# Token mixing in scaled float16 pairs, two of three score sets joined, and early blocks split 5, 4, 3

## The chip, the cores and the metric

One core of a Trainium2 chip runs the whole kernel. The metric is the time on the device in microseconds (us); the kernel before takes 724.33 us (median of three runs, 723.59 to 726.13).

## What is computed

Four batches of 576 tokens, eight heads of 64 channels. Forget-gated causal attention is followed by a mixer (over tokens, then over channels) and by a gated feed-forward with a convolution of three taps along the tokens. Cut to what matters:

```python
scores = q @ k.T / sqrt(64) + (cum[:, None] - cum[None, :])     # cum: running sum of log f; causal
attn = exp(scores - max) / (sum + 1e-9)
x = concat_heads(attn @ v)                                      # 4 x 576 x 512
h = relu(x.T @ w_tok1) @ w_tok2                                 # token mixing: 576 -> 256 -> 576
u = x + h.T
x2 = u + relu(u @ w_ch1) @ w_ch2                                # channel mixing: 512 -> 1536 -> 512
hh = relu(x2 @ w_in)                                            # 512 -> 1024
out = (hh * sigmoid(conv3(hh))) @ w_out
```

The weights come as float64 and are turned into float32 on the chip. The results have to hold to about float32, so most products are made of pairs: a value is split into a high and a low part of 16 bits (or of TensorE's reduced 32-bit format, float32r), and three matmuls (high by high, high by low, low by high) stand for one.

## The kernel before, in words

**The order is planned.** The program adds tasks (engine, estimated time, rank, what it reads and writes) to a list scheduler, `Order`. It takes, again and again, the task that can begin first by its estimates, and among those that can begin at once the one with the lowest rank. The result is one fixed order for each engine, and each engine then waits in that order for real. A rank is thus a priority. `PER` is the step of rank from one head to the next; weights, loads and groups have ranks relative to heads. Channel mixing on TensorE has a rank of 1000 and more, so it fills what the attention leaves free.

**Attention** (32 heads, `pair(p)` for two heads at a time, lines 1031 to 1088). `score` makes three sets of row blocks for both heads: block 4; blocks 0 and 3; blocks 1 and 2. Products of 64 rows in float32 are followed by one product that adds the decay. The result lies in the PSUM ring "z", which has two slots: the set of block 4 takes both (one per head), each other set takes one. VectorE's `smax` (line 912) reads a slot, adds the mask, takes the maximum and so frees it; ScalarE's `sexp` (line 918) makes the exponential. The first 8 heads and the last are transposed by TensorE (line 951), the others by the DMA from float16 pairs: GpSimd makes the high part (`ph`, line 927), VectorE the low part (`pl`, line 933). `pv` multiplies by v (line 983 in float32 for the first 8 heads, lines 988 to 990 in pairs later); `norm` and `xout` (lines 992 to 1007) give x.

**Token mixing** runs once for each group of 4 heads, 8 groups in all (`group(g)`, line 1169). ScalarE and GpSimd split x into `xh` and `xl` in float32r. `t1` makes two results with 15 matmuls of 256 columns each, `t1_hi` and `t1_lo` split them, and `t2` makes four results, each from three transposes of x (the residual, `t2_x`, line 1128) and six matmuls of 288 columns. ScalarE copies each to `us`. All pair matmuls go through the helper `mm3` (lines 278 to 280). The token weights go through `weight` (line 326): load, decode on ScalarE and VectorE (lines 315, 319, 320), a high part on ScalarE, a low part on GpSimd.

**Channel mixing.** After two groups a batch is complete: the largest of u (`um`), a scale (`su`), float16 pairs `uh` and `ul`, and then a first part of the 12 blocks of 128 hidden channels, `PARTS_M[0] = 4` of them, can run while attention goes on with the next batch. The parts of 5 and of 3 blocks, and the feed-forward, follow after attention. The weights of a part are loaded and decoded, their squares summed for a scale (`weight_set`, line 407) and split (lines 467 and 471). v is scaled from group 2 on by a power of two from the sum of its magnitudes (`v_abs`, `v_sum`, `v_pow`).

Of the kernel before, what the change touches and what calls it, by code (L numbers as in the profile page):

```python
# [143 lines left out]
def fox_moe_kernel(  # L144
# [14 lines left out]
    nc = tc.nc  # L159
# [35 lines left out]
    PARTS_M = (4, 5, 3)  # L195
# [13 lines left out]
    SETR = ((-25.0, 0.0),)  # L209
    LATER = (-60.0, 0.0, 20.0)  # L210
    PER = 5.0
# [112 lines left out]
    def weight(block, place, rank, key, pools_=(), copy=None):  # L324
# [51 lines left out]
        T("POOL", 0.1 + 1.3 * k, rank, low, reads=[c, (key, "h")], writes=[key], pools=pools_)  # L376

# [286 lines left out]
    with tc.manual_schedule():  # L664
# [114 lines left out]
        def v_abs(g):  # L779
# [7 lines left out]
        def v_sum(g):  # L787
            ps = bank("w")[:, 0:1]
            nc.tensor.matmul(ps, ones.to_broadcast([128, 128]), vs_t[g], start=True, stop=True)
            vps_t[g] = ps  # L790

        def v_pow(g):
            sc = ap1.tile([128, 2], F32, tag="vsc", name="vsc", bufs=3)
            nc.vector.tensor_scalar(sc[:, 0:1], vps_t[g], 2.0 ** -86, None, ALU.max)
            si = sc[:, 0:1].bitcast(I32)
            nc.vector.tensor_scalar(si, si, 0x7F800000, 0x7F800000, ALU.bitwise_xor, ALU.bitwise_and)
            nc.vector.tensor_scalar(sc[:, 0:1], sc[:, 0:1], 8192.0, None, ALU.mult)
            nc.vector.tensor_scalar(sc[:, 1:2], sc[:, 0:1], PSC * 1e-9, 2.0 ** -125, ALU.mult, ALU.max)
# [18 lines left out]

        def v_tasks(g, rank):
# [4 lines left out]
            if HG * g < FULL:  # L823
                if g:
                    T("SP", 2.0, rank - 6, load_v32, g, writes=keys, moved=3.0, pools=["a3"])
                return
# [3 lines left out]
            kw = turn("w")  # L830
            junk = ("junk",)
            T("ACT", 1.27, rank, v_abs, g, reads=[vf], writes=[junk, ("vacc", g % 2)], pools=A2)
            T("PE", 0.2, rank, v_sum, g, reads=[("vacc", g % 2)], writes=[kw], pools=["a1"], ring=[kw])
            T("DVE", 0.5, rank, v_pow, g, reads=[kw], writes=[("vsc", g % 3)], pools=["a1"], ring=[kw])
# [8 lines left out]
        w1h = ap1.tile([128, NS, TOK], F32R, tag="w1h", name="w1h", bufs=1)  # L843
        w1l = ap1.tile([128, NS, TOK], F32R, tag="w1l", name="w1l", bufs=1)
        nc.gpsimd.memset(f32(w1h[64:128, 0]), 0.0)
# [648 lines left out]
```

## Time and profile before

| | us |
|---|---|
| median of the runs (lowest to highest) | 724.33 (723.59 to 726.13) |
| the profiled execution, its own time | 724.63 |
| its span, first to last instruction | 722.9 |
| TensorE matmuls busy | 701.9 (97%) |
| VectorE busy | 507.7 (70%) |
| ScalarE busy | 418.0 (58%) |
| GpSimd busy | 214.2 (30%) |

In the profile PE is TensorE's matmul side, PEld its weight loads, DVE VectorE, ACT ScalarE, POOL GpSimd and SP the engine that issues the DMAs. The duration of a matmul in the trace includes its way through the array; consecutive matmuls overlap, and what one costs in a stream is the distance from its start to the next start.

### The profile page before, as it was taken

The page shows a single profiled execution, that of the slowest core. Times are in us where ns is not written, and L with a number is a line of the kernel's source. Part 1 is how long each engine was busy: PE and PEld are TensorE (multiplying, and loading weights), DVE is VectorE, ACT ScalarE, POOL GpSimd, SP SyncE. Part 2 cuts the span into 40 slices and gives each one's busy share as a digit, 9 for nine tenths or more (in the row PEclk, how much of TensorE's full clock was granted, in tenths as well). Part 3 has the DMA queues.
Part 4 walks back from the last instruction along what each step waited for, and adds up shares of the span by engine and source line. Part 5 has one row for each costly group of instructions (what it writes and reads, how often), then busy time and mean ns, then how long its engine had stood idle before and what let it go on. Part 6 is the DMA issues. An engine that isn't in the chain of part 4 may idle for free.

```text
span 722.9 us, 16264 instructions
## 1 busy us (share of the span) xinstructions
PE 701.9 (97%) x6399; PEld 570.5 (79%) x6399; DVE 507.7 (70%) x1226; ACT 418.0 (58%) x921; POOL 214.2 (30%) x272
## 2 busy tenths in 40 slices
PE   7999879999999999999999999999999999999998
PEld 6888857768787888878878787778877778778786
DVE  6778999899877795375758566335668866975570
ACT  6878685665756454476645443112168766776672
POOL 2351564564264541400001103011013323322230
PEclk9999999999999999999999999999999999999999
DMA  9546898998999597974557644054111111100101
GB/s 214 165 142 218 189 234 162 250 224 211 222 209 178 107 236 164 314 214 145 163 150 210 196 156 151 15 170 126 35 66 50 50 54 47 51 25 26 34 18 50
DMA packets 152973, 101.98 MB, mean 141 GB/s; under 512 B 89984, under 2 KB 145024, under 8 KB 152896
## 3 DMA queue, kind: packets, MB, share of 16 engines
q1 hardware_dynamic: 152896, 100.94, 54.2%
q8 instruction: 50, 0.82, 0.5%
q14 instruction: 27, 0.22, 0.1%
HBM read 57.73 MB, written 23.59 MB: 113 GB/s over the span
## 4 chain that ended last, share of the span: by engine, by line
PE 81%; DVE 11%; ACT 2%; issue 2%; DMA 1%; POOL 1%; SPq 0%; DVEq 0%; POOLq 0%; ACTq 0%
PE w L279 14%; PE w L278 14%; PE w L280 13%; PE z L279 9%; PE z L280 9%; PE z L278 9%; PE z L894 5%; DVE pl L933 3%; PE w L983 3%; DVE t L912 2%; PE w L1128 1%; DVE w L320 1%; PE z L898 1%; PE w L988 1%; PE w L989 1%
## 5 line engine op out<-in xcount | busy, mean ns | idle before, releaser
L278 PEld LDWEIGHTS <-w 128*128 128x128 f16 x1280 | 125.3, 98 | 35.3 <-issue 4.1
L280 PEld LDWEIGHTS <-w 128*128 128x128 f16 x1280 | 125.4, 98 | 34.0 <-issue 2.3
L279 PEld LDWEIGHTS <-w 128*128 128x128 f16 x1280 | 125.1, 98 | 31.2 <-issue 0.4
L279 PE MATMUL w<-ul,w 128*128 128x288 f16 x384 | 110.1, 287 | 2.1 <-DVE ul L510 2.1
L278 PE MATMUL w<-uh,w 128*128 128x288 f16 x384 | 110.0, 287 | 0.3 <-ACT uh L507 0.3
L280 PE MATMUL w<-uh,w 128*128 128x288 f16 x384 | 110.0, 286 | 0.0
L1394 DVE SCALAR_TENSOR_TENSOR cv<-hp,cw,cv 128x286 f32<-128x286 f32 (+1 forms) x128 | 75.0, 592 | 37.9 <-ACT cv L1388 35.6
L273 POOL TENSOR_TENSOR g<-sg,g 128x286 f16<-128x286 f32 (+1 forms) x64 | 55.1, 867 | 156.5 <-ACT g L267 154.8
L559 ACT ACTIVATE r<-w 128x288 f16<-128x288 f32 x96 | 39.1, 408 | 101.5 <-PE w L280 101.2
L918 ACT ACTIVATE t<-t,m 128x192 f32<-128x192 f32 (+4 forms) x160 | 81.3, 553 | 17.3 <-DVE m L912 16.6
L912 DVE CUSTOM_DVE_ANT_0 t<-z,mask 128x192 f32<-128x192 f32 (+4 forms) x160 | 70.3, 478 | 10.1 <-PE z L898 10.0
L563 DVE SCALAR_TENSOR_TENSOR r<-w,r 128x288 f16<-128x288 f32 x96 | 43.4, 454 | 45.9 <-ACT r L559 45.0
L279 PE MATMUL z<-g,w 128*128 128x286 f16 (+1 forms) x256 | 73.3, 286 | 0.0
L278 PE MATMUL w<-vh,w 128*128 128x288 f16 x256 | 73.2, 286 | 0.0
L279 PE MATMUL w<-vl,w 128*128 128x288 f16 x256 | 73.2, 286 | 0.0
L280 PE MATMUL w<-vh,w 128*128 128x288 f16 x256 | 73.2, 286 | 0.0
L278 PE MATMUL z<-r,w 128*128 128x288 f16 x256 | 73.2, 286 | 0.0
L279 PE MATMUL z<-r,w 128*128 128x288 f16 x256 | 73.2, 286 | 0.0
L280 PE MATMUL z<-r,w 128*128 128x288 f16 x256 | 73.2, 286 | 0.0
L278 PE MATMUL z<-g,w 128*128 128x286 f16 (+1 forms) x256 | 73.0, 285 | 0.0
L280 PE MATMUL z<-g,w 128*128 128x286 f16 (+1 forms) x256 | 72.9, 285 | 0.0
L636 POOL TENSOR_TENSOR p<-p,u 128x288 f32<-128x288 f32 x32 | 26.1, 847 | 157.3 <-DMA p<-p_d 90.8
(181 smaller groups left out, 1660.6 us busy)
## 6 DMA issues: line engine op xcount, KB each, us to landing
wraw<-in_moe_w_ch_dram SPq DMA_DIRECT2D x24, 512.0 KB, 4.7
qk<-in_qk_dram SPq DMA_DIRECT2D x16, 608.0 KB, 5.2
u_d<-us SPq DMA_DIRECT2D x8, 576.0 KB, 3.8
p_d<-res SPq DMA_DIRECT2D x32, 144.0 KB, 3.3
p<-p_d SPq DMA_DIRECT2D x8, 576.0 KB, 5.0
u<-u_d SPq DMA_DIRECT2D x8, 576.0 KB, 5.2
x_d<-p SPq DMA_DIRECT2D x8, 576.0 KB, 3.1
u<-x_d SPq DMA_DIRECT2D x8, 576.0 KB, 4.0
```

Of the source, the lines that this page charges most:

```text
L273: nc.gpsimd.tensor_tensor(o, a, b, ALU.subtract)
L278: nc.tensor.matmul(ps, wh, xh, start=(first and i == 0), stop=False)
L279: nc.tensor.matmul(ps, wh, xl, start=False, stop=False)
L280: nc.tensor.matmul(ps, wl, xh, start=False, stop=(last and i == n - 1))
L559: nc.scalar.activation(out=t[:, 0, :], in_=box["z", m], func=AF.Relu)
L563: nc.vector.scalar_tensor_tensor(t[:, 1, :], box["z", m], 0.0, f32(t[:, 0, :]), ALU.max, ALU.subtract)
L636: nc.gpsimd.tensor_tensor(box["p"][:, d], box["p"][:, d], box["u"][:, d], ALU.add)
L894: nc.tensor.matmul(out_[x], t[r, Q0[i]:Q0[i] + 128], t[r, k0:k0 + n], start=first, stop=False)
L912: nc.vector.tensor_tensor_reduce(to, z_t.pop((n, i)), mk, -0.125, 3e38, ALU.add, ALU.min, m_t[n][0:rows, i:i + 1])
L918: nc.scalar.activation(out=tt[0:rows, o:o + w], in_=tt[0:rows, o:o + w], func=AF.Exp, bias=m_t[n][0:rows, i:i + 1], scale=-1.0)
L933: nc.vector.scalar_tensor_tensor(l_t[n][:, sl], t_t[n % TB][:, sl], PSC, h_t[n][:, sl], ALU.mult, ALU.subtract)
L1394: nc.vector.scalar_tensor_tensor(cv, hp_t[m][:, s0 + t:s1 + t], cw[:, t, m:m + 1], cv, ALU.mult, ALU.add)
```

## The change

- The token weights and x, and what lies between the two token matmuls, become float16 pairs instead of float32r. float16 has little range, so the weights are scaled: a new `tok_set` decodes them, sums their squares on ScalarE, spreads the sums with one small matmul per block, makes a power of two on VectorE, and scales each block on GpSimd before it is split.
- v gets a scale for the first two groups too (`v_scales`), from squares; the scale stays in x. The residual x is brought to the scale of the token product by `x_scale` on GpSimd (32 times, before the transposes that read it), and `u_copy` takes the scale out again with a factor that `u_back` makes.
- The sets (0, 3) and (1, 2) of the scores are joined: the first takes the z slots of both, and the second has the rank -1000000, so that it follows at once.
- `PARTS_M` goes from 4, 5, 3 to 5, 4, 3; `PER` from 5 to 7; the ranks of weights move, as do some of the planner's estimates.

The diff, cut to its core:

```diff
-    PARTS_M = (4, 5, 3)
+    PARTS_M = (5, 4, 3)
...
-    SETR = ((-25.0, 0.0),)
+    TOKR, TOKP = 4.0, 5.0
+    VRANK = 10.0
+    SETR = ((-15.0, 20.0),)
     LATER = (-60.0, 0.0, 20.0)
-    PER = 5.0
+    PER = 7.0
...
+    def tok_set(name, blocks, slots, places, ranks, cranks, factor):
...
+            def squares(k=k, i=i, p=p, n=n):
+                nc.scalar.activation(out=box[k][0:p, 0:n, 1].bitcast(F32), in_=WT[i][0:p, 0:n], func=AF.Square,
+                                     accum_out=stat[0:p, k:k + 1])
...
+            def scaled(i=i, p=p, n=n):
+                nc.gpsimd.tensor_scalar(WT[i][0:p, 0:n], WT[i][0:p, 0:n], pw[0:p, 0:1], 0.0, ALU.mult, ALU.add)
...
+            T("SP", 0.4, ranks[k] - 8, load, writes=[w if plain else a], moved=0.3 + 1.5 * f * p / 128)
+            if not plain:
+                T("ACT", 0.15 + 0.5 * f, ranks[k], exp, reads=[a], writes=[w])
+                T("DVE", 0.15 + 1.1 * f, ranks[k], dec, reads=[w], writes=[a, w])
+                T("ACT", 0.25 + 0.65 * f, ranks[k], squares, reads=[w], writes=[a, ("stat", name, k)])
...
+        T("PE", 0.12 + 0.11 * nb, cranks[0], span, reads=[("stat", name, k) for k in range(nb)], writes=[kw], ring=[kw])
+        T("DVE", 0.6 + 0.13 * nb, cranks[0], scale, reads=[kw], writes=[("pw", name)], ring=[kw])
+        for k, f, w, key, scaled, high, low in fns:
+            T("POOL", 0.2 + 0.5 * f, cranks[k], scaled, reads=[("pw", name)], writes=[w])
+            T("ACT", 0.15 + 0.5 * f, cranks[k], high, reads=[w], writes=[(*key, "h")], pools=["a1"])
+            T("POOL", 0.1 + 1.3 * f, cranks[k], low, reads=[w, (*key, "h")], writes=[key], pools=["a1"])
...
-            nc.scalar.activation(out=junk, in_=v_t[g].rearrange("p a n -> p (a n)"), func=AF.Abs, accum_out=acc)
+            if HG * g < FULL:
+                nc.scalar.activation(out=junk.rearrange("p (a h d) -> p a h d", a=NS, h=HG),
+                                     in_=vp32_t[g % 2][:, 0:NS, :, 0:64], func=AF.Square, accum_out=acc)
+            else:
+                nc.scalar.activation(out=junk, in_=v_t[g].rearrange("p a n -> p (a n)"), func=AF.Square, accum_out=acc)
...
-            ps = bank("w")[:, 0:1]
-            nc.tensor.matmul(ps, ones.to_broadcast([128, 128]), vs_t[g], start=True, stop=True)
-            vps_t[g] = ps
+        def v_span(g):
+            vps_t[g] = spread(vs_t[g], 1)
...
+            power_of_root(sc, vps_t[g], 128, 8.0 if HG * g < FULL else 4096.0)
...
-        w1h = ap1.tile([128, NS, TOK], F32R, tag="w1h", name="w1h", bufs=1)
+        w1h = ap1.tile([128, NS, TOK], F16, tag="w1h", name="w1h", bufs=1)
...
+        JOINED = ((0, 3), (1, 2))
...
-                tok[g][name] = ap1.tile([128, NS, HG * D], F32R, tag=name, name=name)
+                tok[g][name] = ap1.tile([128, NS, HG * D], F16, tag=name, name=name)
...
+        def x_scale(n):
+            nc.gpsimd.tensor_scalar(x_of(n), x_of(n), tac[:, 0:1], 0.0, ALU.mult, ALU.add)
+
+        PE_S = {(4,): 1.65, (0, 3): 1.25, (1, 2): 1.25}
...
-                kz = [turn("z") for _ in range(2 if blocks == (4,) else 1)]
-                T("PE", PE_S[blocks], t0 + 1, score, p, blocks, reads=[kq], writes=[*kz, ("scores",)], pools=A2 + A1,
-                  ring=kz)
+                second = blocks == JOINED[1]
+                kz = [turn("z") for _ in range(2 if blocks == (4,) else 1)] if not second else [kj]
+                if blocks == JOINED[0]:
+                    kj = turn("z")
+                T("PE", PE_S[blocks], -1e6 if second else t0 + 1, score, p, blocks, reads=[kq], writes=[*kz, ("scores",)],
+                  pools=A2 + A1, ring=kz + [kj] if blocks == JOINED[0] else kz)
...
+                T("POOL", 0.6, rank + 7, x_scale, n, reads=[("tac",)], writes=[("xf", g % 2, n % HG)], pools=A1)
...
-            act_cast(st["u"][:, d, e * CH:(e + 1) * CH], st["ps2", d, e])
+            nc.scalar.activation(out=st["u"][:, d, e * CH:(e + 1) * CH], in_=st["ps2", d, e], func=AF.Copy, scale=st["back"])
+
+        def u_back(g):
+            t = ap1.tile([128, 1], F32, tag="ub", name="ub", bufs=2)
+            nc.gpsimd.tensor_scalar(t, vs_t[g][:, 1:2], tac[:, 1:2], 1.0 if HG * g < FULL else 512.0, ALU.mult, ALU.mult)
+            tok[g]["back"] = t
...
-                T("PE", 1.8, t0 + 3, t1, g, a, reads=[*xk, *W1K], pools=A1, ring=[kw],
+                T("PE", 1.66, t0 + 3, t1, g, a, reads=[*xk, *W1K], pools=A1, ring=[kw],
...
-                    T("PE", 1.42, t0 + 4, t2, g, d, e, writes=[kw, *(uk if first else [("us", g % 2, d, e)])], pools=A1, ring=[kw],
+                    T("PE", 1.17, t0 + 4, t2, g, d, e, writes=[kw, *(uk if first else [("us", g % 2, d, e)])], pools=A1, ring=[kw],
...
-        for k, (block, hi, lo) in enumerate(tok_w):
-            weight(block, lambda hi=hi, lo=lo: (hi, lo), 10 + 5.0 * k, ("tokw", k), pools_=["a1"])
+        for name, ws, slots, q, factor in (("t1", tok_w[:3], (9, 10, 11), TOKR, 4.0),
+                                           ("t2", tok_w[3:], (9, 10, 11, 12), TOKR + 15.0, 2.0 ** 13)):
+            n = len(ws)
+            tpw.append(tok_set(name, [w[0] for w in ws], slots, [w[1:] for w in ws], [q + TOKP * k for k in range(n)],
+                               [q + TOKP * n + TOKP * k for k in range(n)], factor))
...
-                                [q + 2.5 * k for k in range(n)], [q + 2.5 * n + 2.5 * k for k in range(n)], factor)
+                                [q + 2.0 * k for k in range(n)], [q + 2.0 * n + 2.0 * k for k in range(n)], factor)
```

## Rows read from the trace of the kernel before

**Rows 1.** The page: busy time of each engine, and the chain by engine.

```profile
PE 701.9 (97%) x6399; PEld 570.5 (79%) x6399; DVE 507.7 (70%) x1226; ACT 418.0 (58%) x921; POOL 214.2 (30%) x272
PE 81%; DVE 11%; ACT 2%; issue 2%; DMA 1%; POOL 1%; SPq 0%; DVEq 0%; POOLq 0%; ACTq 0%
```

**Rows 2.** Busy time by stretch: length, busy us (instructions) by engine, clock, DMA.

```profile
20.00:82.00 62.00, 60.42 (x493) 52.88 (x492) 49.36 (x144) 48.98 (x109) 25.30 (x30) 1.00 0.56 170
82.00:112.00 30.00, 23.86 (x266) 20.04 (x265) 28.33 (x74) 20.24 (x42) 15.48 (x18) 0.94 0.95 230
112.00:310.00 198.00, 192.20 (x2199) 157.81 (x2196) 155.09 (x410) 115.92 (x249) 93.28 (x106) 1.00 0.93 204
310.00:719.50 409.50, 409.49 (x3340) 326.82 (x3340) 261.64 (x558) 218.37 (x493) 75.25 (x90) 1.00 0.32 96
```

**Rows 3.** TensorE's waits, the whole span: engine, line, for whom; us, times, longest.

```profile
PE z L894 <- DVE m L912: 5.0, 8, 1.3
PE w L258 <- DVE um L264: 2.6, 2, 2.4
PE w L279 <- DVE ul L510: 2.1, 1, 2.1
```

**Rows 4.** Timeline of TensorE, token matmuls of 256 columns in float32r (start, duration).

```profile
87.47 0.28 PE L278 MATMUL w<-xh,w1h 128*128 128x256 f32 x1
...
90.32 0.28 PE L278 MATMUL w<-xh,w1h 128*128 128x256 f32 x1
```

**Rows 5.** Timeline of TensorE, float16 matmuls of 288 columns.

```profile
116.07 0.29 PE L278 MATMUL w<-uh,w 128*128 128x288 f16 x1
...
119.01 0.29 PE L278 MATMUL w<-uh,w 128*128 128x288 f16 x1
```

**Rows 6.** Timeline of TensorE, the four results of `t2` of one group, first to last.

```profile
93.17 0.58 PE L1128 MATMUL w<-ident,xf 64*128 64x64 f32 x3
93.51 0.38 PE L278 MATMUL w<-w2h,t1h 128*128 128x288 f32 x1
...
98.03 0.20 PE L988 MATMUL w<-vp,pt 128*128 128x65 f16 x1
```

**Rows 7.** Timeline of TensorE, score sets apart, each with the row that follows it.

```profile
143.38 1.25 PE L894 MATMUL z<-qk 64*128 64x64 f32 x8
...
144.79 0.55 PE L1128 MATMUL w<-ident,xf 128*128 128x128 f32 x3
...
146.07 1.13 PE L894 MATMUL z<-qk 64*128 64x192 f32 x8
...
147.37 0.38 PE L789 MATMUL w<-vacc,ones 128*128 128x1 f32 x2
```

**Rows 8.** Timeline of TensorE, the same sets in one stretch, up to 93.17 [rows 6].

```profile
90.77 1.25 PE L894 MATMUL z<-qk 64*128 64x64 f32 x8
```

**Rows 9.** Groups by line: the small matmuls of `um`; xcount, busy us, mean ns.

```profile
L258 PE MATMUL w<-ident,um 128*128 128x128 f32 x16 | 3.2, 305 | 2.6 <-DVE um L264 2.6
```

**Rows 10.** Line 471 (splitting weights) on VectorE, in 82 to 112 us.

```profile
82.00:112.00 30.00, 3.20 (x4) 0.94 0.95 230
```

**Rows 11.** Timeline of VectorE and GpSimd: the same operation alone and beside GpSimd.

```profile
109.81 0.81 DVE L933 SCALAR_TENSOR_TENSOR pl<-t,ph 128x640 f16<-128x640 f32 x1
120.46 1.65 DVE L933 SCALAR_TENSOR_TENSOR pl<-t,ph 128x640 f16<-128x640 f32 x1 [0.25 <-POOL ph L927]
118.64 4.05 POOL L927 TENSOR_SCALAR ph<-t 128x640 f16<-128x640 f32 x3 [0.21 <-ACT t L918]
```

**Rows 12.** Groups by line on GpSimd: the form nearest to the new operation.

```profile
L927 POOL TENSOR_SCALAR ph<-t 128x640 f16<-128x640 f32 x23 | 23.6, 1027 | 10.2 <-ACT t L918 10.2
```

**Rows 13.** The start: second `qk` issue, loads by line (us to landing), TensorE's second pair.

```profile
7.31 0.60 SPq L692 DMA_DIRECT2D qk<-in_qk_dram  x1
...
qk<-in_qk_dram SPq DMA_DIRECT2D x16, 608.0 KB, 5.2
...
14.39 1.24 PE L894 MATMUL z<-qk 64*128 64x288 f32 x7
```

More of the change, by code (lines that the diff above doesn't have):

```diff
@@ L816, in v_part, with v_scales @@
                 pool_cast(hi, t)
+        def v_scales(g, rank, reads, pools_):
+            kw = turn("w")
+            T("ACT", 1.27, rank, v_squares, g, reads=reads, writes=[("junk",), ("vacc", g % 2)], pools=pools_)
+            T("PE", 0.25, rank, v_span, g, reads=[("vacc", g % 2)], writes=[kw], pools=["a1"], ring=[kw])
+            T("DVE", 0.7, rank, v_pow, g, reads=[kw], writes=[("vsc", g % 3)], pools=["a1"], ring=[kw])
         def v_tasks(g, rank):
@@ L825, in v_tasks @@
                     T("SP", 2.0, rank - 6, load_v32, g, writes=keys, moved=3.0, pools=["a3"])
+                v_scales(g, rank + VRANK, keys, ["a3", "a1"])
                 return
@@ L829, in v_tasks @@
             T("SP", 1.1, rank - 6, load_v, g, writes=[vf], moved=3.2, pools=A2)
[L830 to L834, printed above, removed]
+            v_scales(g, rank, [vf], A2)
             T("ACT", 1.37, rank, v_scale, g, reads=[("vsc", g % 3)], writes=[vf], pools=A2)
@@ L1083, in pair @@
                       pools=["a3"], ring=[kw])
-                T("DVE", 0.5, rank + 6, norm, n, reads=[kw] + ([] if n < FULL else [("vsc", g % 3)]), writes=[("rs", n % 2)], pools=A1, ring=[kw])
+                T("DVE", 0.5, rank + 6, norm, n, reads=[kw, ("vsc", g % 3)], writes=[("rs", n % 2)], pools=A1, ring=[kw])
                 T("DVE", 0.46, rank + 6, xout, n, reads=[kw, ("rs", n % 2)], writes=[("xf", g % 2, n % HG)], pools=A1, ring=[kw])
@@ L1225, in back_task, with tok_scales @@
               reads=[("scale", id(su[b])), ("pw", f"c1{part}"), ("pw", f"c2{part}")])
-        W1K = [("tokw", k) for k in range(3)]
-        W2K = [("tokw", k) for k in range(3, 7)]
+        W1K = [("tokw", "t1", k) for k in range(3)]
+        W2K = [("tokw", "t2", k) for k in range(2 * KT)]
         v_tasks(0, -8)
-        AVAIL = [(H * (b + 1) - 1) * PER + 35 for b in range(B)]
+        AVAIL = [(H * (b + 1) - 1) * PER + 40 for b in range(B)]
         LATE = 1000.0
-        for k, (block, hi, lo) in enumerate(tok_w):
-            weight(block, lambda hi=hi, lo=lo: (hi, lo), 10 + 5.0 * k, ("tokw", k), pools_=["a1"])
+        tpw = []
+        for name, ws, slots, q, factor in (("t1", tok_w[:3], (9, 10, 11), TOKR, 4.0),
[3 more added lines that the diff above has]
+                               [q + TOKP * n + TOKP * k for k in range(n)], factor))
+        def tok_scales():
+            for x, (bound, op) in enumerate(((2.0 ** 60, ALU.min), (2.0 ** -60, ALU.max))):
+                nc.vector.tensor_scalar(tac[:, x:x + 1], tpw[0][:, x:x + 1], tpw[1][:, x:x + 1], bound, ALU.mult, op)
+        T("DVE", 0.2, TOKR + 15.0 + TOKP * 4, tok_scales, reads=[("pw", "t1"), ("pw", "t2")], writes=[("tac",)], pools=["a1"])
         t0 = AVAIL[0] - 30
```

85 lines of the change are left out of this document (64 added, 21 removed).

## The prediction

> **What bounds the kernel now.** I read the page first: TensorE's matmuls are busy for 701.9 of 722.9 us, and four fifths of the chain that ends last are TensorE's own instructions [rows 1]. So the time is the sum of TensorE's work plus 21.0 us in which it idles. Then the busy times by stretch [rows 2]: from 310 us to 719.5 us it never idles, and from 20 to 82 us for 1.6 us only. Idle time lies at the start and the end (some 7.5 us together, 62.0 - 60.4 and the like taken off), in 82 to 112 us (6.1 us), and in small pieces in 112 to 310 us (5.8 us). In 82 to 112 us VectorE is busy for 28.3 of 30 us: there the first batch's u has to be finished before channel mixing can fill anything, and VectorE is late. The list of waits names the same: 2.6 us for `um` and 2.1 us for `ul`, one time each in the main, and 5.0 us in eight waits for a z slot that `smax` has not freed [rows 3]. The clock of that stretch is 0.94 on the mean [rows 2]; as it is either 1.2 or 2.4 GHz, some 12% of 30 us ran at half speed, which costs about 1.8 us more. After 310 us only less TensorE work can help; before it, less work or less waiting.
>
> **The change part by part.**
>
> *Token matmuls, `t1`.* In float32r 24 steps of 256 columns take 2.85 us, 0.119 us each [rows 4]. A float16 stream of 288 columns steps by 0.1225 us [rows 5]. No row shows float16 at 256 columns. By columns it is 0.1225 x 256 / 288 = 0.109 us; at worst it is that of the 288 columns, a loss of 0.004. I take 0.109, as a stream this long is paid by columns. There are 8 groups x 30 = 240 of them: 240 x 0.010 = 2.4 us saved (0.9 lost to 2.4), and on TensorE's path, since it is nearly always busy there. Each `t1` also no longer has to change from float16 work to 32-bit and back; unseen alone, 0 to 0.1 us for each of 16, I take 0.8. Sum 3.2 us.
>
> *Token matmuls, `t2`.* Four results take 93.17 to 98.03, 1.215 us each; the three transposes ahead of the first take 0.34 [rows 6] and stay as they are. With six float16 steps a result is 0.34 + 6 x 0.1225 = 1.075 us. The upper bound is today's 1.215, if the change from transposes to float16 eats the gain. I take 1.13, nearer to the sum, since six of nine instructions have a row. 32 results x 0.085 = 2.7 us (0 to 4.5).
>
> *Joined scores.* Apart, the two sets take 143.38 to 144.79 and 146.07 to 147.37, 1.41 + 1.30 = 2.71 us [rows 7]; in one stretch 90.77 to 93.17, 2.40 us [rows 6, 8]. The saving is 0.3 us, but the trace has them joined already in 7 of 16 pairs; I count 9 x 0.25 = 2.2 us. The price is in waiting: a joined pair needs both z slots before it begins, see the rivals.
>
> *Added on TensorE.* `tok_set` spreads 7 columns of sums, `v_scales` one column for each of 8 groups where 6 products stood: 9 more columns. The nearest row has 8 columns in 3.2 us, 0.4 each [rows 9], part of which is the way through the array that a neighbour covers. I take 0.27 x 9 = 2.4 us (1 to 3.6).
>
> Sum on TensorE: -3.2 - 2.7 - 2.2 + 2.4 = -5.7 us (-9 to +1).
>
> *Five blocks first instead of four.* Channel mixing has the same matmuls in all. One block costs 24 x 0.1225 = 2.9 us per chunk of half a batch; eight chunks move 23.5 us from the stretch without idle time into or right behind the attention. In itself that is 0. It gives more filler to 112 to 310 us: per batch 5.9 us more TensorE work against some 1 us of VectorE's (`rl`), so VectorE gets slack. It also brings one more block of each weight ahead, with its load on the DMA queue, its decode and its split on ScalarE and VectorE.
>
> *Ranks.* In 82 to 112 us VectorE splits the second set of weights for 3.2 us [rows 10], and decodes more of it. Now that set has ranks of 79 and more beside 59 for the group that completes the batch, where before it was 40 to 60 beside 45: it goes behind. In the same way `pl` of the next head had rank 44 beside 45 for `um` and now has 60 beside 59. So `um`, `su` and `ul` come several us earlier on VectorE. What is late next is the chain itself: copy, largest, spread, scale, split, which no rank shortens. I take 4 us of the 7.9 us (6.1 idle, 1.8 clock) as regained (0 to 7). The weights that go behind meet VectorE again in 112 to 310 us, where it is busy for 155 of 198 us; there I leave the 5.8 us of idle time as they are (3 to 9).
>
> *GpSimd.* `x_scale` adds 32 operations of 320 elements; the row of the same form has 640 elements in 1.03 us [rows 12], so they take 0.5 to 1.0 us, I take 0.65: 21 us on an engine that is busy for 134 of the 290 us from 20 to 310 us [rows 2]. Queued behind each on GpSimd are `ph` and `xl`; `pl` on VectorE and the DMA transposes wait for `ph`. `t2` waits for `x_scale` of the last head, but `t1` (3.3 us) lies between, which covers it; without that cover it would be 0.65 us for each of 8 groups. `u_back`, and the scaling of seven weight blocks, are covered in the same way.
>
> The row on what that does to VectorE: `pl` of 640 elements takes 0.81 us at 109.81, and 1.65 us at 120.46 while GpSimd runs `ph` from 118.64 to 122.69 [rows 11]. The Trainium skill, "SBUF — State Buffer", section "Who interferes with whom", says that a VectorE instruction with two SBUF inputs contends with a GpSimd instruction that reads SBUF; the trace agrees. That is a rule against this change, and I price it as a rival from those rows.
>
> *VectorE and ScalarE otherwise.* `v_pow` grows by some small operations per group and the squares of nine blocks are new on ScalarE (busy for 49 of 62 us in 20 to 82 us [rows 2]). TensorE is full there with the first eight heads, so I cost them at nothing; if the token weights were late by more than the work that TensorE has in hand, each us would show.
>
> *The start.* The second `qk` load was issued at 7.31 us, lands 5.2 us later on the median, and is used at 14.39 us [rows 13]: 1.9 us to spare. Its rank is now 5, behind the first two token loads with -4 and 1, which are 64 x 256 x 8 and 128 x 512 x 8 bytes. At the 230 GB/s of a busy stretch [rows 2] 655 KB take 2.8 us. So about 1 us is lost (0 to 3).
>
> **How the sum stands.** The profiled execution took 724.6 us, 0.3 over the median. 724.6 - 5.7 - 4 + 1 = 715.9 us, or 715.6 beside the median.
>
> **The rivals.**
>
> 1. *TensorE's work falls, the idle time stays.* VectorE is busy for 94% of 82 to 112 us, and a queue that is full stays late if ranks only shuffle it. For it: later stretches carry what is moved. Against: 3.2 us of splitting are not needed there. 724.3 - 5.7 + 1 = 719.6 us.
> 2. *GpSimd slows VectorE.* 21 us of `x_scale`, of which about a quarter would meet an operation with two SBUF inputs (`pl`, decode and splits are about that share of VectorE's time after 82 us): 5 us more on VectorE. If all of it reached TensorE: 715.6 + 5 = 720.6 us. Against: the three waits for VectorE of [rows 3] are 8 + 2 + 1 = 11 times.
> 3. *float16 is no faster than float32r, and the changes of type cost as much.* The change then doesn't do what it says on TensorE: -2.2 + 2.4 in work, with the 4 us regained and 1 lost, 721.5 us. Against: the steps in rows 4 and 5.
> 4. *Most idle time goes.* With more filler and a better placed batch end 8 us more than forecast at most are to be had; at 6 us, 709.6 us.
> 5. *Slower: the z slots.* Joined sets begin only when `smax` has freed both slots, and so does block 4 of the next pair. From pair 4 to 15 that is 24 starts in TensorE's fixed order, beside a VectorE that is 78 to 94% busy. The eight waits of today are 0.63 us each [rows 3]. If all 24 starts wait that long, it is 15 us where 5.0 are now: 715.6 + 10 = 725.7, and with 0.75 us each 728.6 us. It decides the sign from (8.7 + 5.0) / 24 = 0.57 us per start. Against: the planner knows of both slots and can put channel mixing ahead.
>
> **How the numbers follow.** Forecast 0.48; rival 1 0.22; rival 2 0.08; rival 3 0.05; rival 4 0.10; rival 5 0.07. About 0.3% (2.2 us) is what a measurement can tell from no change. Rival 5 lies above 726.5 for most of its share and within the band for the rest; rivals 2 and 3 lie near the band's edge at 722.1 and spill into it with a quarter. So slower 0.05, same 0.08, faster 0.87. The range takes in rival 4 and rivals 1 to 3 with their bounds, 708 to 723 us, and leaves out rival 5 and a little at both ends.
>
> **What the profile after would show.** `t1` in steps of 0.109 us and `t2` results of 1.13 us or less; each pair's two sets in 2.4 to 2.5 us; TensorE busy for about 696 us; in the stretch before the first channel mixing less idle time than 6 us, with waits for `um` and `ul` shorter; no first `qk` wait beyond 2 us. The prediction is wrong if waits for z slots grow well past 5 us, if `pl` and the decodes are slower on the mean, or if the token products of group 0 wait for their weights.

## The result, and the profile after

| | before | after |
|---|---|---|
| median of the runs, us (lowest to highest) | 724.38 (six runs beside after's) | 718.13 (717.27 to 720.02, six runs) |
| ratio of after to before | | 0.9906 (95% interval 0.9882 to 0.9930) |
| the profiled execution, us | 724.63 | 717.27 |
| its span, us | 722.9 | 715.5 |
| TensorE matmuls busy, us | 701.9 | 695.6 |
| TensorE idle, span less busy, us | 21.0 | 19.9 |

The change makes the kernel 6.3 us faster: in the range, 2.5 us above the forecast of 715.6. The page of after, busy times and the chain by engine (answers [rows 1]):

```profile
PE 695.6 (97%) x6417; PEld 560.0 (78%) x6417; DVE 506.0 (71%) x1264; ACT 427.8 (60%) x939; POOL 242.3 (34%) x321
PE 88%; DVE 7%; ACT 2%; issue 1%; SPq 1%; POOL 1%; DMA 0%; ACTq 0%; POOLq 0%; DVEq 0%
```

TensorE's busy time falls by 6.3 us (the forecast's sum: 5.7), its idle time by 1.1 us only. Where, the busy times by stretch tell. Columns: stretch, its length, busy us (instructions) of PE, PEld, DVE, ACT, POOL, clock, DMA share, GB/s. First the start of the kernel before, then after (answers [rows 2]):

```profile
0.00:20.00 20.00, 15.89 (x110) 12.94 (x110) 13.28 (x46) 13.94 (x30) 4.94 (x29) 1.00 0.95 228
```

```profile
0.00:20.00 20.00, 13.73 (x75) 11.01 (x77) 12.52 (x44) 12.47 (x27) 5.09 (x31) 0.91 0.91 224
20.00:82.00 62.00, 62.00 (x538) 55.00 (x534) 46.55 (x166) 52.77 (x122) 31.32 (x46) 1.00 0.48 149
82.00:112.00 30.00, 23.11 (x222) 17.26 (x221) 27.57 (x64) 22.88 (x44) 17.94 (x22) 0.89 0.83 216
112.00:310.00 198.00, 194.71 (x2311) 155.64 (x2310) 159.99 (x439) 120.05 (x254) 111.61 (x119) 1.00 0.93 206
```

Idle time, length less PE: 4.1 to 6.3 us in the first 20; 1.6 to none in 20 to 82; 6.1 to 6.9 in 82 to 112, at a lower clock (0.94 to 0.89); 5.8 to 3.3 in 112 to 310. So the batch end, from which the forecast took 4 us, gave nothing back. With the clock it costs more than before: by these rows half speed cost up to 1.8 us there before (30 us at 0.94) and up to 3.3 us after (30 us at 0.89), and up to 1.8 us in the first 20 us after (0.91), none before. TensorE's waits over the whole span (engine, line, for whom; us, times, longest; answers [rows 3]):

```profile
PE w L260 <- ACT junk L869: 3.1, 1, 3.1
PE w L281 <- DVE ul L594: 1.7, 1, 1.7
PE w L281 <- POOL xl L275: 1.7, 2, 1.3
PE z L987 <- DVE m L1005: 1.6, 2, 0.9
PE w L260 <- ACT junk L872: 1.3, 2, 1.0
```

The waits for z slots fell from 5.0 us in eight to 1.6 in two. New at the top is the wait of 3.1 us for `junk` of L869: the squares of v for the first two groups, which had no scale before. The squares for the later groups (L872) stand where the magnitudes of v stood, for which TensorE waited 0.8 us before.

### The profile page after: what moved, and what is told of

Same layout as the page of the kernel before. It is cut to its first block, busy times and chain, and to the rows that moved or that the text cites. A ratio compares the mean times of both kernels' runs of the same rounds, so it can differ in the third digit from the quotient of the medians.

```text
span 715.5 us, 16392 instructions
## 1 busy us (share of the span) xinstructions
PE 695.6 (97%) x6417; PEld 560.0 (78%) x6417; DVE 506.0 (71%) x1264; ACT 427.8 (60%) x939; POOL 242.3 (34%) x321
## 4 chain that ended last, share of the span: by engine, by line
PE 88%; DVE 7%; ACT 2%; issue 1%; SPq 1%; POOL 1%; DMA 0%; ACTq 0%; POOLq 0%; DVEq 0%
PE w L280 15%; PE w L281 15%; PE w L282 15%; PE z L281 8%; PE z L280 8%; PE z L282 8%; PE z L987 6%; PE w L1076 3%; PE w L1228 2%; PE w L1044 2%; DVE pl L1026 2%; PE z L991 1%; PE w L260 1%; DVE ul L594 1%; PE w L1082 1%; PE w L1081 1%
## 5 line engine op out<-in xcount | busy, mean ns | idle before, releaser
L280 PE MATMUL w<-uh,w 128*128 128x288 f16 x416 | 119.6, 288 | 2.0 <-ACT uh L591 1.1
L281 PE MATMUL w<-ul,w 128*128 128x288 f16 x416 | 119.7, 288 | 1.7 <-DVE ul L594 1.7
L282 PE MATMUL w<-uh,w 128*128 128x288 f16 x416 | 119.6, 288 | 0.0
L720 POOL TENSOR_TENSOR p<-p,u 128x288 f32<-128x288 f32 x32 | 26.7, 864 | 149.1 <-DMA p<-p_d 89.7
L280 PE MATMUL w<-vh,w 128*128 128x288 f16 x224 | 64.1, 286 | 0.0
L281 PE MATMUL w<-vl,w 128*128 128x288 f16 x224 | 64.1, 286 | 0.0
L282 PE MATMUL w<-vh,w 128*128 128x288 f16 x224 | 64.1, 286 | 0.0
L280 PE MATMUL z<-r,w 128*128 128x288 f16 x224 | 64.1, 286 | 0.0
L281 PE MATMUL z<-r,w 128*128 128x288 f16 x224 | 64.1, 286 | 0.0
L282 PE MATMUL z<-r,w 128*128 128x288 f16 x224 | 64.1, 286 | 0.0
```

The source lines that it names most:

```text
L280: nc.tensor.matmul(ps, wh, xh, start=(first and i == 0), stop=False)
L281: nc.tensor.matmul(ps, wh, xl, start=False, stop=False)
L282: nc.tensor.matmul(ps, wl, xh, start=False, stop=(last and i == n - 1))
L720: nc.gpsimd.tensor_tensor(box["p"][:, d], box["p"][:, d], box["u"][:, d], ALU.add)
```

## The experiments

All runs at a glance. Idle is span less busy; clock is the mean granted clock of the profiled execution. Beside the experiments the kernel before took 725.5 to 725.6 us, so compare rows by their ratios. Two profiles show the slowest execution of their run, over 5 us above its median: v's load in the plan with the ranks of after (744.81 us), and v's squares later (724.74 us).

| | median us | ratio to before (95%) | span | PE busy | idle | clock |
|---|---|---|---|---|---|---|
| before | 724.38 | | 722.9 | 701.9 | 21.0 | 0.997 |
| after | 718.13 | 0.9906 (0.9882 to 0.9930) | 715.5 | 695.6 | 19.9 | 0.993 |
| *order kept:* before, float16 alone | 722.44 | 0.9959 (0.9942 to 0.9977) | 719.5 | 698.3 | 21.2 | 0.993 |
| before, 7 more pairs joined | 725.53 | 0.9992 (0.9973 to 1.0011) | 724.1 | 703.4 | 20.7 | 0.991 |
| after, v's squares later | 718.82 | 0.9916 (0.9883 to 0.9949) | 723.0 | 701.7 | 21.3 | 0.981 |
| after, `x_scale` twice | 717.57 | 0.9889 (0.9867 to 0.9910) | 714.9 | 696.4 | 18.5 | 0.993 |
| *planned anew:* before, joined | 731.34 | 1.0073 (1.0050 to 1.0097) | 729.7 | 704.9 | 24.8 | 0.983 |
| after, v's load in the plan | 739.27 | 1.0185 (1.0147 to 1.0223) | 742.9 | 712.0 | 30.9 | 0.970 |
| after, first set earlier | 744.66 | 1.0264 (1.0238 to 1.0289) | 744.2 | 707.6 | 36.6 | 0.974 |
| after, sets apart | 738.62 | 1.0176 (1.0152 to 1.0201) | 736.6 | 707.8 | 28.8 | 0.981 |
| after, ranks of before | 741.24 | 1.0239 (1.0206 to 1.0273) | 738.2 | 703.0 | 35.2 | 0.979 |
| *ranks searched anew:* v's load in the plan | 714.56 | 0.9855 (0.9826 to 0.9883) | 712.3 | 694.2 | 18.1 | 0.997 |
| the same, sets apart | 726.41 | 1.0017 (0.9995 to 1.0039) | 724.2 | 703.3 | 20.9 | 0.988 |
| the same, parts 4, 5, 3 | 725.63 | 1.0006 (0.9992 to 1.0020) | 723.3 | 700.4 | 22.9 | 0.991 |

My theory after the result was the forecast's: less TensorE work, and waits that can be taken away one by one. The runs of the next section were made on it.

### One wait or one part, planned anew

The v load told to the planner, so that v's squares don't go ahead of the joined scores:

```diff
+                if not g:
+                    T("-", 6.0, -1e6, lambda: None, writes=keys)
                 if g:
                     T("SP", 2.0, rank - 6, load_v32, g, writes=keys, moved=3.0, pools=["a3"])
```

> The changed kernel, with one thing other: the plan takes the first load of v to land 6 us after its start, so the squares of v for group 0 and the product that spreads them come later in each engine's order. Theory: in the changed kernel that product stands ahead of the joined score sets of the first pair and TensorE waits 3.1 us there for ScalarE, with its clock at 0.91 of full speed over the first 20 us; without it the time falls from 718.1 to 713.5 to 715.5 us and the first 20 us show a clock near 1.0. Rival: the start is bound by the loads and by ScalarE's own work, and the wait only moves to the next score set: 717 to 718.5 us.

The score sets apart again, the rest as in after:

```diff
-                second = blocks == JOINED[1]
...
+                kz = [turn("z") for _ in range(2 if blocks == (4,) else 1)]
```

> The changed kernel with the score sets (0, 3) and (1, 2) apart again, and the planner's estimates for them as before. Theory: joining saves 0.2 to 0.3 us for each pair that would run apart and costs nothing in waiting (waits for z slots are 1.6 us in the changed kernel, 5.0 before), so apart it takes 2 to 4 us more: 720 to 722 us. Rival: the joined sets hold up TensorE at both z slots, and the fall in waits comes from the other parts; apart it is the same or faster, 716 to 718.5 us.

The kernel before with joined sets and nothing else:

```diff
-                kz = [turn("z") for _ in range(2 if blocks == (4,) else 1)]
...
+                second = blocks == JOINED[1]
...
+                T("PE", PE_S[blocks], -1e6 if second else t0 + 1, score, p, blocks, reads=[kq], writes=[*kz, ("scores",)],
```

> The kernel before with the joined score sets alone (and the planner's estimates for them). Theory: scores take 2 to 3 us less on TensorE and nothing else changes: 721 to 722.5 us where the kernel before takes 724.4. Rival: without the other parts, joined sets wait for both z slots beside a VectorE that is 94% busy; waits for z slots grow past 5 us and the time is 724 to 728 us.

The first weight set's ranks earlier, out of 82 to 112 us:

```diff
-    SETR = ((-15.0, 20.0),)
+    SETR = ((-45.0, 20.0),)
```

> The changed kernel with the first set of channel weights at ranks 30 lower, so that its decode and split come well before the first batch is complete. Theory: in the changed kernel VectorE splits this set between 82 and 112 us (5.2 us there, 3.2 before), which is why the 6.9 us of idle time there did not shrink; moved ahead, the stretch regains 2 to 4 us with its clock: 714 to 716.5 us. Rival: the idle time there is the chain of copy, largest, scale and split itself, which no rank shortens: 717.5 to 719 us.

Measured: 739.27, 738.62, 731.34 and 744.66 us, all slower than before, where 713.5 to 722.5 were expected. The edits are small; what they set off isn't. Each goes through the list scheduler, which turns a shifted task into another order for the whole attention. The waits of the four, in this order:

```profile
PE z L989 <- DVE m L1007: 9.1, 4, 3.7
```

```profile
PE z L987 <- DVE m L1005: 10.2, 4, 4.5
```

```profile
PE z L895 <- DVE m L913: 5.5, 4, 2.7
PE w L258 <- DVE stat_c L451: 4.7, 2, 2.9
```

```profile
PE z L987 <- DVE m L1005: 14.1, 3, 6.1
```

The wait for a z slot, rival 5's mechanism, comes in three or four long pieces instead of eight short ones, with the sets joined (9.1 and 14.1 us) as well as apart (10.2 us). So each of these runs measures its edit together with the order that it sets off, and can't price the edit by itself. The theory that waits can be taken away one by one fell here.

### One part, order kept

The next runs leave the order as the planner made it, and move tasks by hand at most. First float16 for the token matmuls alone, in the kernel before (without the scales):

```diff
-        w1h = ap1.tile([128, NS, TOK], F32R, tag="w1h", name="w1h", bufs=1)
+        w1h = ap1.tile([128, NS, TOK], F16, tag="w1h", name="w1h", bufs=1)
...
```

> The kernel before with the token weights, x and what lies between the token matmuls in float16 instead of float32r, without any scale, and with every engine's order as it was. Theory: the two token products alone are worth 2.4 + 0.8 + 2.7 = 5.9 us of TensorE's time, and with the order kept they show in full where TensorE is always busy: 718 to 720.5 us where the kernel before takes 724.4 to 725.5. Rival: in the fixed order TensorE then waits at the next z slot or for x, since VectorE's and ScalarE's work sets the pace there: 723 to 725 us.

Then seven of the nine pairs of score sets that stand apart in the kernel before, put side by side in its finished order:

```diff
+        for p in range(16):
...
+            order.remove(k2)
+            order.insert(order.index(k1) + 1, k2)
```

> The kernel before in its own order, only that in 7 of the 9 pairs whose score sets (0, 3) and (1, 2) stood apart they now stand next to one another on TensorE, after both z slots are free (in the other two pairs that can't be done without moving other work). Theory: 7 x 0.25 = 1.7 us less on TensorE; waits for z slots stay below 6 us: 722 to 724.5 us. Rival: each moved set waits for VectorE, 0.5 us and more for each: 726 to 731 us, as in the kernel whose plan was made anew with joined sets alone (731.3).

Float16: 722.44 us, 3.2 us less than the run of before beside it, and between what the theory (718 to 720.5) and the rival (723 to 725) expected. Added up over the span (from each stretch's first start to the next stretch's, idle time taken off), the token matmuls and their transposes take 64.7 us instead of 70.4: 5.7 us less, as forecast (5.9). A little over half of it shows. Where the rest goes is seen in 82 to 112 us of this run:

```profile
82.00:112.00 30.00, 24.56 (x264) 19.42 (x265) 28.18 (x72) 19.79 (x40) 15.19 (x16) 0.83 0.97 233
```

and in its wait for `um` (2.6 us in [rows 3]):

```profile
PE w L258 <- DVE um L264: 3.3, 2, 3.1
```

TensorE comes to the batch's end earlier, waits longer for VectorE, and the mean clock of the stretch is 0.83 where it was 0.94. The first product of channel mixing starts at 105.69 us, at 105.39 us in the kernel before: what was saved ahead of that point is not there behind it. The other executions agree: at a mean clock of 0.992 or 0.993 this form took 721.0 to 721.7 us and the kernel before, at 0.993, 726.1 us on the median, 4.9 us more; but no execution of this form had a clock above 0.993, where 10 of 23 of the kernel before had 0.995 and more.

Joined pairs: 725.53 us, no gain; the expectation of 722 to 724.5 failed. The rival's 726 to 731 did not come either: with the order kept joining costs no waiting for z slots (5.0 us in eight before):

```profile
PE z L909 <- DVE m L927: 4.9, 7, 1.3
```

PE's busy time even rose by 1.5 us, at a clock of 0.991 instead of 0.997. An estimate from those rows takes span x (1 - clock) as the upper end of what half speed cost: 6.5 us here and 2.2 in before; taken off the busy times, 696.9 and 699.7 us, 2.8 us less work. Executions of the same clock don't bear that out: at 0.998 the joined form took 723.10 and 723.65 us, the kernel before 723.54 and 723.97. So the estimate takes too much off, the gain at the same clock is some 0.4 us, and why the expected 1.7 us don't show stays open.

### The start

In after, TensorE's queue has the product of v's squares (`v_span(0)`) ahead of the first pair's joined scores. The timeline of TensorE (start, duration), kernel before, then after:

```profile
9.99 1.25 PE L894 MATMUL z<-qk 64*128 64x64 f32 x8 [0.97 <-DVE m L912]
...
12.50 1.97 PE L951 MATMUL w<-ident,t 128*128 128x128 f32 x16
```

```profile
12.11 0.49 PE L260 MATMUL w<-ident,vacc 128*128 128x128 f32 x2 [3.07 <-ACT junk L869]
12.53 2.27 PE L987 MATMUL z<-qk 64*128 64x64 f32 x8
...
16.70 0.55 PE L1044 MATMUL w<-ident,t 128*128 128x128 f32 x3
```

After the wait the two sets take 4.17 us (12.53 to 16.70) instead of 2.51, because most of that time runs at half clock, 1.2 instead of 2.4 GHz. One microsecond of it, columns as above, with a clock of 0.50:

```profile
13.00:14.00 1.00, 1.00 (x8) 0.60 (x7) 0.90 (x6) 0.04 (x1) 0.00 (x0) 0.50 1.17 279
```

The scores of the first pair end 4.2 us later. In the next run the three tasks of v's scale stand later in after's order:

```diff
+        for name, args, after in (("v_squares", (0,), ("sexp", 1, 4)), ("v_span", (0,), ("ptr", 0, 1)), ("v_pow", (0,), ("v_span", 0))):
+            k = order.pop(at(name, *args))
+            order.insert(at(*after) + 1, k)
```

> The changed kernel in its own order, only that the squares of v for group 0, their spread on TensorE and the power of two on VectorE stand further back: the squares behind the exponential of block 4 of head 1, the spread behind the second transposes of head 0. Theory: the 3.1 us in which TensorE waits there and most of the slow clock of the first 20 us go: 713.5 to 715.5 us where the changed kernel takes 718.1. Rival: the wait moves on to the joined sets' slots and to ScalarE, which is no earlier: 717 to 719 us.

718.82 us (716.84 to 724.74, the profiled execution being the 724.74): as after. The scores do run from 9.74 us at full clock, and then TensorE waits elsewhere, twice, at the transposes that need ScalarE's exponentials (wait, then the timeline). The first time v's squares stand ahead of them on ScalarE; the second time, at 18.04 us, ScalarE itself waits for VectorE:

```profile
PE w L1051 <- ACT t L1018: 4.3, 2, 2.3
```

```profile
14.87 0.66 PE L1051 MATMUL w<-ident,t 128*128 128x128 f32 x4 [1.97 <-ACT t L1018]
...
18.04 1.30 PE L1051 MATMUL w<-ident,t 128*128 128x128 f32 x5 [2.29 <-ACT t L1018]
```

By its time the rival held: the 3.1 us were not to be had by moving that wait alone. The trace is that of the slowest execution; where the five faster ones wait is not shown.

### GpSimd

`x_scale` a second time, with a factor of 1:

```diff
             nc.gpsimd.tensor_scalar(x_of(n), x_of(n), tac[:, 0:1], 0.0, ALU.mult, ALU.add)
+            nc.gpsimd.tensor_scalar(x_of(n), x_of(n), 1.0, 0.0, ALU.mult, ALU.add)
```

> The changed kernel in its own order, with each of the 32 scalings of x on GpSimd done twice (the second time by one): some 25 us more on GpSimd, 20 us of them beside VectorE's operations with two SBUF inputs or before t2. If contention with GpSimd costs TensorE time in the changed kernel (my rival 2, priced at up to 5 us), the same again is added: 721 to 723 us. Theory: it is covered, 718 to 719.5 us.

717.57 us, where the theory had 718 to 719.5 and the rival 721 to 723. GpSimd's groups by line (xcount, busy us, mean ns), the first of after, the second the added one:

```profile
L1121 POOL TENSOR_SCALAR xf<-xf,tac 128x320 f32<-128x320 f32 x32 | 24.9, 780 | 2.8 <-DVE tac L1348 0.8
```

```profile
L1122 POOL TENSOR_SCALAR xf<-xf 128x320 f32<-128x320 f32 x32 | 17.8, 557 | 2.7
```

17.8 us more on GpSimd (25 were expected) cost VectorE 1.6 us (506.0 to 507.6 busy) and the kernel nothing. Rival 2 fell, as far as a second dose of that size can tell.

### Ranks searched for the form

What was left to explain is why the whole change gains 6.3 us when, of its parts, float16 alone gains 3.2 us, joining alone nothing, and each edit planned anew loses. Theory: the smaller work shows in an order that keeps TensorE fed, and the ranks, the five blocks and the joined sets together give one. So three forms were run with ranks searched anew for each, by the end that the kernel's planner estimates, and with v's load in the plan; and the whole change with the old ranks. Each search is a search: a better order of the apart form or of parts 4, 5, 3 may exist.

```diff
-    TOKR, TOKP = 4.0, 5.0
-    VRANK = 10.0
+    TOKR, TOKP = -2.0, 5.0
+    VRANK = 22.0
...
-    LATER = (-60.0, 0.0, 20.0)
+    LATER = (-60.0, -10.0, 20.0)
...
-                                [q + 2.0 * k for k in range(n)], [q + 2.0 * n + 2.0 * k for k in range(n)], factor)
+                                [q + 2.75 * k for k in range(n)], [q + 2.75 * n + 2.75 * k for k in range(n)], factor)
```

> The change with one thing told to the planner, that the first v load lands at 6 us (until then it thought v was there at 0), and with ranks searched anew for that: the second weight set's rank steps from 2.0 to 2.75, token weights from rank 4 to -2, the start's v scale from 10 to 22, the third head's offset from 0 to -10. Theory (the first wait for v, 3.1 us, is real, and a list of tasks whose ranks suit it can take it out; that the same edit with the old ranks cost 15 us was the order, not the edit): 712 to 716 us, ratio to the kernel before 0.982 to 0.987, TensorE busy for 695 to 697 us, idle 16 to 19 us. Rival (the idle time at the start and the batch end is data that is not there yet; what one order avoids another one waits for elsewhere, as when v's squares were moved by hand): 717 to 720 us.

The same with the sets apart:

```diff
-    SETR = ((-15.0, 20.0),)
-    LATER = (-60.0, 0.0, 20.0)
+    SETR = ((-20.0, 20.0),)
+    LATER = (-60.0, -20.0, 20.0)
...
-                second = blocks == JOINED[1]
...
```

> The change with the score sets (0, 3) and (1, 2) apart as before, the planner's estimates for them the measured 1.41 and 1.30 us, the v load told to it, and ranks searched anew for this form. The run with the sets apart and the change's own ranks took 738.6 us, which is an order without fit as much as a price of the sets. Theory (joining is worth some 3 us of TensorE work and no more, if each form has ranks that suit it): 718 to 723 us, TensorE busy 698 to 700 us. Rival (joining saves nothing at all, as in the kernel before where seven more joined pairs left the time as it was): within 1 us of the joined form with searched ranks that runs beside it. Second rival (without joining no order is good): over 730 us.

And with the parts of before:

```diff
-    PARTS_M = (5, 4, 3)
+    PARTS_M = (4, 5, 3)
...
-    SETR = ((-15.0, 20.0),)
-    LATER = (-60.0, 0.0, 20.0)
+    SETR = ((-10.0, 5.0),)
+    LATER = (-30.0, 10.0, 0.0)
```

> The change with the parts of channel mixing 4, 5, 3 as before, the v load told to the planner, and ranks searched anew for this form. Theory (five blocks ahead give attention more filling work, which takes idle time out of 112 to 310 us and costs nothing in work): 719 to 726 us, that is 5 to 10 us over the form with five blocks and searched ranks beside it, with TensorE's work within 1 us of that form's and its idle time longer by the difference. Rival (moving a block is neutral, as the forecast's sum had it): within 2 us of that form.

Old ranks, the change otherwise whole:

```diff
-    SETR = ((-15.0, 20.0),)
+    SETR = ((-25.0, 0.0),)
...
-    PER = 7.0
+    PER = 5.0
...
-        AVAIL = [(H * (b + 1) - 1) * PER + 40 for b in range(B)]
+        AVAIL = [(H * (b + 1) - 1) * PER + 35 for b in range(B)]
...
```

> The change whole, but with the ranks of the kernel before: head step 5 instead of 7, the first part's weight set from -25 and 0 instead of -15 and 20, the batch's offset 35 instead of 40, weight steps 2.5 instead of 2. Theory (less TensorE work shows only in an order that keeps TensorE fed, and the ranks make it): 736 to 745 us, slower than the kernel before by 12 to 20 us, TensorE busy 695 to 698 us and idle 40 to 48 us. Rival (the smaller work shows whatever the ranks, and the ranks add the forecast's 4 us at the batch end): 718 to 723 us.

The first of the four took 714.56 us, 3.6 us under after's median and the fastest of all; by the ratios the two intervals just touch. Its stretches:

```profile
0.00:20.00 20.00, 15.35 (x100) 12.41 (x100) 14.06 (x48) 14.63 (x33) 5.11 (x31) 1.00 0.97 244
82.00:112.00 30.00, 24.31 (x277) 18.67 (x277) 29.28 (x68) 20.36 (x41) 17.88 (x23) 0.94 0.82 200
112.00:310.00 198.00, 193.86 (x2264) 155.06 (x2262) 155.43 (x431) 120.83 (x257) 108.82 (x128) 1.00 0.91 208
```

The start is back at full clock with 4.65 us idle (after: 6.3), the batch end has 5.7 us idle at 0.94 (after: 6.9 at 0.89). The wait for v's squares at the start is 0.8 us instead of 3.1. So the edit that made after 21 us slower under its own ranks goes with a gain of some 3 us under ranks that suit it. How much of the gain is the edit and how much the searched ranks is not shown: the ranks without the edit were not run.

Apart took 726.41 us, outside the expected 718 to 723, 11.9 us over the joined form; neither rival fits. Parts 4, 5, 3 took 725.63 us, in the expected 719 to 726, but 11.1 us over where 5 to 10 were expected; of that 4.8 us are idle time and the rest is busy time, not idle time alone as the theory had it. The stretch from 112 to 310 us, apart first:

```profile
112.00:310.00 198.00, 191.41 (x2235) 150.38 (x2235) 164.86 (x437) 121.35 (x252) 106.95 (x117) 0.98 0.94 209
```

```profile
112.00:310.00 198.00, 187.96 (x2187) 151.07 (x2183) 157.46 (x423) 119.19 (x253) 109.76 (x126) 0.98 0.90 207
```

Their waits for z slots, in the same order, and last that of the joined form with five blocks:

```profile
PE z L989 <- DVE m L1007: 9.5, 8, 2.4
```

```profile
PE z L989 <- DVE m L1007: 9.5, 6, 3.3
```

```profile
PE z L989 <- DVE m L1007: 3.7, 3, 1.8
```

With four blocks ahead 10.0 us of 112 to 310 us are idle, with five 4.1. The matmuls of channel mixing and of the feed-forward's first weights take the same in both forms (379.3 and 379.6 us net of idle time): as work the block is neutral, as forecast, and as filler it isn't. By the estimate above, half speed costs up to 8.7 us in the apart form, 6.5 us with parts 4, 5, 3 and 2.1 us with both; the work is then 694.6, 693.9 and 692.1 us, which would make joining worth some 2.5 us of work. That estimate took too much off above, and here too the clock alone can't be the rest: at a mean clock of 0.991 the apart form took 725.1 to 728.4 us and parts 4, 5, 3 took 724.7 to 725.4, while the joined form with five blocks took 715.0 and 715.1 at 0.992. So joined sets and five blocks are each worth 11 to 12 us under ranks searched for each form, as far as the searches go; how that divides into work, waiting and clock is not shown.

Old ranks: 741.24 us, as the theory had it, with less idle and more busy time than expected (35.2 and 703.0 us), at a clock of 0.979. The waits:

```profile
PE w L260 <- ACT junk L872: 10.2, 2, 9.3
PE z L987 <- DVE m L1005: 6.9, 2, 4.2
```

The change with the ranks of before is 23 us slower than with its own, and slower than the kernel before. One wait of 9.3 us, for the squares of v of a later group, is the largest piece. The old ranks were not made for a plan with scaled token weights and five blocks, so the run prices them for this change and says nothing of them in general.

## Why the prediction was right, and where it was not

The forecast and the measured time differ by 2.5 us, but the parts differ by more, and that they cancel is luck. The forecast had 5.7 us less work, 4 us less idle time and low clock at the batch end, 1 us lost at the start, and nothing elsewhere. Measured, busy time fell by 6.3 us, although the lower clock took up to 3.3 us of that again. Idle time at the batch end and in the first 20 us grew by 0.8 and 2.2 us. The stretches 20 to 82 and 112 to 310 us, which the forecast left as they were, gave 4.1 us of idle time (1.6 and 2.5).

**Token matmuls: right.** The steps are 0.11 us where 0.109 was forecast; timeline of after (answers [rows 4, 6]):

```profile
92.32 0.27 PE L281 MATMUL w<-xl,w1h 128*128 128x256 f16 x1
92.43 0.27 PE L282 MATMUL w<-xh,w1l 128*128 128x256 f16 x1
...
93.46 0.64 PE L1228 MATMUL w<-ident,xf 64*128 64x64 f32 x3
93.93 0.29 PE L280 MATMUL w<-w2h,t1h 128*128 128x288 f16 x1
...
94.67 0.49 PE L1228 MATMUL w<-ident,xf 128*128 128x128 f32 x3
```

Net of idle time `t1` fell from 30.5 to 28.4 us, 2.1 less where 3.2 were forecast, because part of it ran at half clock; in the joined run with searched ranks, where none of it does, it takes 26.7 us, 3.8 less. No run shows by itself the 0.8 us that this forecast held for changes of type. `t2` with its transposes fell from 39.9 to 37.2 (forecast 2.7 less, measured 2.7). Rival 3 fell.

**Joined sets and what was added: right in work.** Scores went from 68.0 to 65.1 us (forecast 2.2 less, measured 2.9), the small products of sums from 8.4 to 10.6 (forecast 2.4 more, measured 2.2). The float16 products with v took 1.9 us less, and channel mixing with the feed-forward's first weights 1.6 us more; neither was forecast. The busy time fell by 6.3 us, forecast were 5.7.

**The batch end: wrong.** "I take 4 us of the 7.9 us as regained" is the step that failed. What it aimed at did come: TensorE's waits for `um` and `ul` in 82 to 112 us fell from 4.5 us to 2.0. But waits for ScalarE and GpSimd took their place, ahead of `t1` (`xh`, `xl`), for v's squares and for `uh`: 5.0 us where they were 1.1. The rows that changed, before, then after (`ul`: 2.1 in [rows 3], 1.7 above):

```profile
PE w L258 <- DVE um L264: 2.4, 1, 2.4
PE w L279 <- POOL xl L273: 0.6, 1, 0.6
PE w L278 <- ACT uh L507: 0.3, 1, 0.3
PE w L789 <- ACT junk L782: 0.2, 1, 0.2
```

```profile
PE w L280 <- ACT xh L269: 1.6, 1, 1.6
PE w L281 <- POOL xl L275: 1.3, 1, 1.3
PE w L280 <- ACT uh L591: 1.1, 1, 1.1
PE w L260 <- ACT junk L872: 1.0, 1, 1.0
PE w L260 <- DVE um L266: 0.3, 1, 0.3
```

As a cause, what I can point to is this: I followed the second weight set behind the batch's end and did not follow the first, whose ranks of 44 to 62 (15 to 32.5 before) put it there instead. VectorE's splits in 82 to 112 us (answers [rows 10], 3.20 in 4):

```profile
82.00:112.00 30.00, 5.20 (x5) 0.89 0.83 216
```

`um` begins at 102.05 us, and the first product of channel mixing at 106.49 (105.39 before). ScalarE has the squares of v for a later group in the same place, but the magnitudes stood there before, as long and at nearly the same time (from 103.33 us before, 103.50 after), so they are not what is new. So rival 1, the idle time stays, describes what happened at the batch end (719.6 by its sum, 718.1 measured). That the first set's place is the cause was not shown on the chip: the run that moved it got another order altogether, and the searched ranks still have 4.18 us of splits there, in 4, with less idle time. This stays open.

**The start: the size within its range, the place wrong.** The 1 us (0 to 3) for the second `qk` load wasn't lost there; TensorE waits for `qk` once, for the first pair, 1.4 us, 1.7 before. The loss was v's squares, which I had put at nothing because TensorE has other work in hand from 20 to 82 us; they are needed before that. It is 0.6 us more idle time over the first 82 us, and 1.7 us more for the scores at half clock.

**112 to 310 us: better than left.** 3.3 us idle instead of 5.8. "In itself that is 0" was true of the work of the five blocks and false of the time, by the run with parts 4, 5, 3 and ranks searched for it.

**GpSimd: covered, as taken.** `x_scale` takes 0.78 us, 0.65 forecast; `pl` of 1024 and of 640 elements takes 1.38 and 1.00 us on the mean, 1.35 and 1.01 before. The Trainium skill, "SBUF — State Buffer", section "Who interferes with whom", has a VectorE instruction with two SBUF inputs contend with a GpSimd instruction that reads SBUF, and single rows do [rows 11]. The sum here doesn't grow by it: VectorE is busy for 506.0 us, 507.7 before, with the decodes shorter on the mean (0.74 us, 0.82 before) and the splits of the channel weights longer (0.92 us, 0.80 before). One such split took 2.27 us at the batch end, beside GpSimd (timelines of VectorE and GpSimd):

```profile
94.40 2.27 DVE L555 SCALAR_TENSOR_TENSOR w<-w,pw_c,w 128x512 f16<-128x512 f32 x1
```

```profile
92.05 4.07 POOL L898 TENSOR_TENSOR vp<-vf,vp 64x256 f16<-64x256 f32 x3
```

**Ranks: mis-sized.** I priced them at the 4 us of the batch end. Taken back alone they cost 23 us. The prediction got the sign because it took the order for as good as the old one; that it would be so could not be read from the profile of before, and was luck.

**The z slots: rival 5 fell** for this order (1.6 us), and joining seven more pairs with the order kept left it at 4.9 us. In the slower orders it is 5.5 to 14.1 us, apart as well as joined: the order sets it, not the joining.

## What to carry to other kernels

Where a list scheduler fixes the order, an edit has two prices: its work, which can be read from rows, and the order it sets off, which can't, and was here up to 26 us for edits worth 3. Measure a part with the order held, and judge a form only with ranks searched for it. Work saved ahead of a point that waits for data on another engine can turn into idle time and a lower clock there, as it did with nearly half of what float16 alone saved; count on it only from behind that point. When a wait is to be shortened, look at what TensorE would wait for next: here 2.5 us less for VectorE became 3.9 us more for ScalarE and GpSimd.

## What the runs showed of the hardware that was not expected

Idle time can be paid twice. After 3.07 us without work the same 20 score matmuls took 4.17 us, 2.51 in the kernel before: for most of it TensorE was granted 1.2 instead of 2.4 GHz. The run with v's load in the plan and the ranks of after does the work of after with 712.0 us of busy time instead of 695.6, at a mean clock of 0.970 instead of 0.993 (in its slowest execution). The Trainium skill, "TensorE: Matmul & The Clock Gate", section "HAM oscillation — how this bites in real kernels", tells the same of a kernel that waits for DMA: waits let the clock fall, and the work behind them starts slow. Not every wait does it here: with 3.3 us of idle time in 112 to 310 us, in pieces of 0.9 us and less, the mean clock of after stays at 1.00 there.

Transposes ahead of float16 cost more than ahead of float32r: from the first of the three to the first of the six products 0.33 to 0.48 us in after's group at 93 us, 0.24 to 0.40 in before, at a granted clock of 1.00 in both; over the span 12.9 and 10.4 us. The six products gain more, 29.5 to 24.3 us. The forecast, which left the transposes as they were, came out right as the sum of the two.

In the run with `x_scale` twice the operation that scales by a value from SBUF took 768 ns on the mean, the one with a constant, right behind it, 557 ns. Which of the two differences makes it is not shown.
